# Linear attention and a gated two-layer product on one core: the openings of the slabs interleaved, the last head pairs of batches 0 and 1 woven into them, batch 1's queries loaded beside w_out

## The chip, the cores and the metric

The kernel runs on one core of a Trainium2 chip. The metric is the device time of one execution in microseconds (us), as the median of several runs. The engines are TensorE (PE), VectorE (DVE), ScalarE (ACT), GpSimd (POOL) and SyncE (SP); each works through its own instructions in order and waits on semaphores for the others.

## The reference

```python
def _attn_ref(q, k, v):                       # (8, 8, 576, 64) each
    q_s = np.exp(q - max over d); q_s /= sum over d
    k_s = np.exp(k - max over s); k_s /= sum over s
    kv = np.einsum('bhsd,bhse->bhde', k_s, v)
    return np.einsum('bhsd,bhde->bhse', q_s, kv)

def _moe_ref(x, w_in, w_out, beta):           # x (4608, 512)
    h = x @ w_in                              # (4608, 2048)
    g = h * (1.0 / (1.0 + np.exp(-beta * h)))
    return g @ w_out                          # (4608, 512)
```

The attention's output is laid out as `(batch * seq, head * d)` and is the `x` of the second part.

## The kernel before, in words

The 4608 tokens are nine slabs of 512. Slab t below 8 holds the first 512 tokens of batch t; slab 8 holds the last 64 tokens of all eight batches. Heads are worked in four pairs (`hp`), and a pair is one of the four 128-row pieces `m` of `x`.

Attention of a batch: `exp_q`, `exp_k`, `exp_kr` on ACT (an Exp table), `norm_main` (a reduction and a reciprocal on VectorE, then a multiplication on VectorE or GpSimd) makes EQ, which is transposed into QT: by TensorE and a copy (`t_steps`) in batches 0 to 2, by a DMA transpose on SP's queue (`norm_turn`, `turn`) later. `cast_v` and `cast_vr` turn V to bf16 with a column of ones. `kv_steps` multiplies EK by VB, then VectorE's reciprocal and `kvd` scale and mask it into KVD. `out_mm` (in `out_step`) multiplies KVD by QT, and ACT or VectorE copies the bank into XT, the `x` of the slab.

The product of a slab has two passes. Pass 1 makes 16 tiles: `pass1_tile` accumulates four matmuls of 128x512 (one for each `m`) in one of three PSUM banks (`HB`, L217), ACT applies Silu into GT and `scale_g` divides by beta on VectorE. Pass 2 of slab 0 is `pass2_group`: 16 pieces `f` times four token groups in banks 3 to 6, copied out by `o2_evac`. Pass 2 of every other slab is `pass2_fast`: a scheme of seven products in place of eight, with sums `g_sum1`, `g_sum2` (GS1, GS2), differences `g_diff`, and `w_sum`, `w_diff` of w_out on VectorE; seven groups of 16 matmuls of 256 columns.

What comes when is written out by hand. Every pass-1 matmul is a slot (`tick`), and pass 2 counts 64 slots more, so a slab has 128; a list `todo` for each slab holds steps of the next batch's attention with the slot at which they are put into TensorE's stream (`attn_late` for batches 2 to 4, `attn` later). In `pass2_fast`, hooks `on(n, ...)` run before the n-th product and put work of other engines (exps, norms, casts, loads) into their queues. In slab 0 the loads, exps, sums and norms of batch 1 are put in front of pass 2:

```python
                load_main("qf", qt_h, QF, 1, split=4, after=P.writer[("wout", 11, 0)])
                ...
                exp_q(1)
                w_sum(0)
                w_sum(2)
                for hp in range(NHP):
                    norm_main(1, hp, 1, POOL if hp else DVE)
                cast_vr_s(1)
```

The weights come in on GpSimd's DMA queue (four w_in parts, then four w_out chunks of four `f`), everything else on SP's. The `warm` matmuls of zeros keep TensorE at work in the head.

Of the kernel before, what the change touches and what calls it, by code (L numbers as in the profile page):

```python
# [8 lines left out]
ALU = mybir.AluOpType  # L9
# [145 lines left out]
def bass_efficient_attn_shen__then__act_swish_beta_kernel(  # L155
# [12 lines left out]
    with ExitStack() as es:  # L168
# [187 lines left out]
        def cast_vr(b, hs=(0, 1)):  # L356
            pi = (b // 2) % 2
            for h in hs:
                o = bass.AP(VR[pi][h], 64 * h * NHP * VW, [[NHP * VW, 64], [VW, NHP], [1, 128]])
                a = bass.AP(VRF, 64 * h * 512, [[512, 64], [128, NHP], [1, 128]])  # L360
                add(POOL, lambda e, o=o, a=a: e.tensor_copy(o, a),
                    r=[("vrf", h), ("vrone", pi, h), ("vr0", pi, h)], w=[("vr", pi, h)])
# [144 lines left out]
        def attn_late(b):  # L507
            x = []
            for hp in range(NHP):
                x += out_step(b, hp, MB, ACTE if hp % 2 else DVE)  # L510
            k01, k23 = kv_steps(b, (0, 1)), kv_steps(b, (2, 3))
            if b == 2:
                s = spread(t_steps(b, (0, 1), MB, ACTE), 104, 107) + spread(k01, 107, 110)
                s += spread(k23, 110, 113) + [(113.5, lambda: g_diff(1))] + spread(x[0:2], 114, 116)
                s += spread(t_steps(b, (2, 3), MB, ACTE), 116.5, 119)
                return s + spread(x[2:4], 122, 125)
            if b == 3:
                s = spread(k01, 97, 101) + spread(k23, 101, 105) + [(105, lambda: g_diff(1))]
                return s + spread(x[0:2], 110, 113) + spread(x[2:4], 120, 123)
            return spread(k01, 93, 97) + spread(k23, 97, 101) + spread(x, 105, 122)  # L520
# [55 lines left out]
        load_win(0, 512)  # L576
        norm_main(0, 2, 1, DVE)
        cast_vr_s(0)
        norm_main(0, 3, 1, POOL)
        for c0 in range(512, DFF, 512):  # L580
            load_win(c0, c0 + 512)
# [20 lines left out]
        exp_k(0, 3, 1)  # L602
        cast_v(0, 3, DVE)
        go(kv_steps(0, (1,), HEAD))
# [3 lines left out]
        warm(2, 0)  # L608
        go(out_step(0, 1, HEAD, ACTE))
        go(kv_steps(0, (3,), HEAD))  # L610
        go(out_step(0, 2, HEAD, ACTE))
        go(out_step(0, 3, HEAD, DVE))
# [6 lines left out]
        def pass1_tile(t, f, tick):  # L619
            bk = HB[hrot[0] % 3]  # L620
            hrot[0] += 1
            x = XT8 if t == 8 else XT[t % 2]
            for m in range(NM):
                rd = [("xt8", p_) for p_ in range(4)] if t == 8 else [("xt", t % 2, m)]
                mm(PS[bk][:, :], WIN[:, m, 128 * f:128 * f + 128], x[:, m, :], m == 0,
                   m == NM - 1, r=rd + [("win", f)], w=[("ps", bk)], bk=bk)
                tick()
            add(ACTE, lambda e: e.activation(GT[:, f, :], PS[bk][:, :], ACT.Silu,  # L628
                                             scale=BETA[:, f:f + 1]),
                r=[("ps", bk), "beta"], w=[("gt", f, 0), ("gt", f, 1)], bank=[bk])  # L630
# [53 lines left out]
        def w_sum(n):  # L684
            x, y = (((0, 0), (1, 1)), ((0, 0), (0, 1)), ((1, 0), (1, 1)))[n]
            add(DVE, lambda e: e.tensor_tensor(WSUM[n][:, :, :], quarter(*x), quarter(*y),  # L686
                                               ALU.add),
                r=wkeys(*x) + wkeys(*y), w=[("ws", n)])
# [7 lines left out]
        def pass2_fast(t, tick, hooks):  # L696
# [25 lines left out]
            def wsum(n):  # L722
                return lambda i: WSUM[n][:, i, :], lambda i: [("ws", n)]
# [40 lines left out]
            if t not in (1, 2):  # L764
                g_diff(0)
                g_diff(1)
# [14 lines left out]
        def pass2_group(t, us, bks, tick):  # L781
            for f in range(NF):
                for u, bk in zip(us, bks):
                    mm(PS[bk][:, :], GT[:, f, 128 * u:128 * u + 128], WOUT[:, f, :], f == 0,
                       f == NF - 1, r=[("gt", f, 0), ("gt", f, 1), ("wout", f, 0), ("wout", f, 1)], w=[("ps", bk)], bk=bk)
                    tick()

        NOW = (0, 1, 2, 7)
        for t in range(NSLAB):
            todo = []  # L790
            if t == 0:
                def one(fn, *a):
                    return lambda: fn(*a)

                def steps(fn, *a):
                    return lambda: go(fn(*a))
                todo = [(x, steps(t_steps, 1, (hp,), NOW, ACTE))
                        for hp, x in enumerate((105, 110, 114, 117))]
                todo += [(104, one(exp_kr_s, 1))]
                todo += [(x, one(exp_k, 1, hp, 1)) for hp, x in enumerate((111, 115, 118, 122))]  # L800
                todo += [(x, one(cast_v, 1, hp, DVE)) for hp, x in enumerate((112, 117.5, 120, 125))]
                todo += [(x, steps(kv_steps, 1, (hp,), NOW))
                         for hp, x in enumerate((116, 119, 124))]
                todo += [(x, steps(out_step, 1, hp, NOW, ACTE)) for hp, x in enumerate((121, 126))]
            elif t < 4:
                todo = attn_late(t + 1)
            elif t < 7:
                todo = attn(t + 1)
                if t > 3:
                    todo += spread(outr_steps(2 * t - 5), *((72, 88), (40, 56), (60, 76))[t - 4])  # L810
            elif t == 7:
                todo = spread(outr_steps(1), 32, 48)
# [8 lines left out]
            if t == 1:  # L821
                cast_vr(2)
                for hp in range(NHP):
                    cast_v(2, hp)
                w_diff(0)
                w_diff(1)
            for n in range(NF + 1):
                if n < NF:
                    pass1_tile(t, n if t == 0 else n // 2 + NG * (n % 2), tick)
                if n:  # L830
                    scale_g(n - 1 if t == 0 else (n - 1) // 2 + NG * ((n - 1) % 2))
# [9 lines left out]
                if t == 1 and n in (2, 5, 8, 11):  # L841
                    o2_evac(0, n // 3, 3 + n // 3, ACTE)
                    if n == 11:
                        store(0)
            if t == 0:
                load_main("qf", qt_h, QF, 1, split=4, after=P.writer[("wout", 11, 0)])
# [5 lines left out]
                w_sum(0)  # L852
                w_sum(2)
                for hp in range(NHP):
                    norm_main(1, hp, 1, POOL if hp else DVE)
                cast_vr_s(1)
                pass2_group(0, (0, 1, 2, 3), (3, 4, 5, 6), tick)
                while todo:
                    todo.pop()[1]()
                go(kv_steps(1, (3,), NOW))  # L860
                go(out_step(1, 2, NOW, ACTE))
                go(out_step(1, 3, NOW, DVE))
# [17 lines left out]
            def casts(b):  # L880
                if b % 2 == 0:
                    cast_vr(b)
                for hp in range(NHP):
                    cast_v(b, hp)

            if t == 1:
                on(0, exps, 2)
                on(0, load, 4)
# [13 lines left out]
            elif t == 3:  # L902
# [3 lines left out]
                on(3, norm_turn, 5, 0)  # L906
                on(4, norm_turn, 5, 2)
# [54 lines left out]
```

## Time and profile before

| | |
|---|---|
| median of 9 runs | 284.74 us (284.08 to 284.93) |
| the profiled execution's own time | 285.0 us |
| its span, first to last instruction | 283.2 us |
| mean granted TensorE clock | 0.999 |
| busy: TensorE, VectorE, ACT, GpSimd | 270.2, 194.8, 186.2, 68.0 us |
| pass 1 of slab 0 begins | 15.83 us |
| slab 1, slab 2, slab 3, slab 4 begin | 50.04, 81.07, 110.80, 140.62 us |
| matmul 128x512 of pass 1, 576 of them | 0.379 us each, overlapping |
| Silu of one tile on ACT, 144 of them | 0.688 us |
| scaling of one tile on VectorE, 144 of them | mean 0.388 us |
| Silu or Exp table load on ACT | 1.283 us |

The span is the time between the first and the last instruction; the device time has a little around it. A matmul's record runs from its start to its modelled end, and the next one starts before that, so the busy share of TensorE is higher than the share of its peak. In the tables of stretches, each row has the length, then for each engine the busy time and the number of instructions, the granted clock, the share of the 16 DMA engines (their overlapping packets can take it past 1) and GB/s.

### The profile page before, as it was taken

How to read it: one execution, taken by the hardware profiler on the slowest of the kernel's cores; microseconds unless marked ns; L12 is line 12 of the kernel's file. 1: busy time of each engine (PE TensorE's matmuls, PEld its weight loads, DVE VectorE, ACT ScalarE, POOL GpSimd, SP SyncE). 2: the span in 40 equal slices, each digit the busy share in tenths (PEclk: the TensorE clock that was granted, in tenths of full speed). 3: DMA queues.
4: the chain of work that ended last, by engine and by line, in shares of the span. 5: the costliest groups of instructions: out<-in, count | busy, mean ns of one | idle time of the engine just before them, and what ended most of it. 6: DMA issues, size and time to landing. Idle time of an engine off the chain costs nothing.

```text
span 283.2 us, 4705 instructions
## 1 busy us (share of the span) xinstructions
PE 270.2 (95%) x1845; PEld 168.2 (59%) x1845; DVE 194.8 (69%) x408; ACT 186.2 (66%) x284; POOL 68.0 (24%) x84
## 2 busy tenths in 40 slices
PE   8999997998999989999899999999999999999994
PEld 2544443447854676458654785478548844874583
DVE  4944484688766798787758795869587649634851
ACT  5787566899378875786777956795675477028610
POOL 2790041060611078200810546004200100000000
PEclk9999999999999999999999999999999999999999
DMA  7999999989991029940499999201800130002005
GB/s 219 315 205 202 236 317 344 241 251 380 325 299 51 0 39 247 298 163 0 76 295 258 319 325 160 94 3 37 241 2 0 21 148 0 2 36 112 2 8 140
DMA packets 57205, 45.39 MB, mean 160 GB/s; under 512 B 26448, under 2 KB 56160, under 8 KB 56160
## 3 DMA queue, kind: packets, MB, share of 16 engines
q1 hardware_dynamic: 52352, 40.38, 50.8%
q0 software_dynamic: 4224, 4.19, 9.0%
q10 hardware_dynamic: 608, 0.53, 0.5%
q8 instruction: 14, 0.23, 0.3%
q14 instruction: 7, 0.06, 0.1%
HBM read 36.71 MB, written 9.44 MB: 163 GB/s over the span
## 4 chain that ended last, share of the span: by engine, by line
PE 71%; DVE 12%; DMA 7%; POOL 6%; ACT 1%; issue 1%; POOLq 0%; DVEq 0%
PE PS L375 40%; PE PS L704 30%; DMA WOUT<-in_moe_w_out_dram 6%; POOL EQ L333 4%; DVE GT L634 2%; DVE QS L331 2%; DVE GS L667 2%; DVE GS L662 2%; DMA QT<-EQ 1%; POOL WIN L549 1%; DVE WSUM L686 1%; DVE GT L674 1%; POOL WOUT L555 1%; ACT GT L628 1%; ACT QT L393 1%
## 5 line engine op out<-in xcount | busy, mean ns | idle before, releaser
L375 PE MATMUL PS<-XT,WIN 128*128 128x512 bf16 x576 | 129.9, 379 | 0.9 <-DVE XT L455 0.8
L628 ACT ACTIVATE GT<-PS,BETA 128x512 bf16<-128x512 f32 x144 | 98.7, 688 | 37.7 <-PE PS L375 37.7
L375 PEld LDWEIGHTS PS<-XT,WIN 128*128 128x128 bf16 x576 | 53.8, 98 | 62.2 <-DVE XT L455 1.9
L634 DVE TENSOR_SCALAR GT<-GT,RB 128x512 bf16<-128x512 bf16 x144 | 53.5, 388 | 39.0 <-ACT GT L628 38.6
L333 POOL TENSOR_TENSOR EQ<-EQ,QI 128x1024 bf16<-128x1024 bf16 (+1 forms) x17 | 29.9, 1758 | 94.0 <-DVE QI L332 73.6
L704 PE MATMUL PS<-WOUT,GT 128*128 128x256 bf16 x256 | 33.6, 273 | 0.0
L704 PE MATMUL PS<-WSUM,GT 128*128 128x256 bf16 x256 | 32.0, 273 | 0.1
L704 PE MATMUL PS<-WOUT,GS 128*128 128x256 bf16 x256 | 30.4, 273 | 0.0
L704 PEld LDWEIGHTS PS<-WSUM,GT 128*128 128x128 bf16 x256 | 24.9, 98 | 4.1 <-issue 0.2
L704 PEld LDWEIGHTS PS<-WOUT,GT 128*128 128x128 bf16 x256 | 24.9, 98 | 3.4
L704 PEld LDWEIGHTS PS<-WOUT,GS 128*128 128x128 bf16 x256 | 24.6, 98 | 3.4
L734 ACT COPY O2S<-PS 128x512 f32<-128x512 f32 x16 | 9.4, 586 | 24.9 <-PE PS L704 22.2
L667 DVE TENSOR_TENSOR GS<-GT 128x512 bf16<-128x512 bf16 (+2 forms) x32 | 22.3, 697 | 0.0
L300 ACT ACTIVATE EQ<-QF 128x512 bf16<-128x512 f32 x32 | 17.9, 619 | 6.0 <-DMA QF<-in_q_dram 5.9
L375 PE MATMUL PS<-VB,EK 128*128 128x129 bf16 x128 | 20.7, 220 | 0.7 <-DVE VB L348 0.5
L331 DVE TENSOR_REDUCE QS<-EQ 128x16 f32<-128x1024 bf16 (+1 forms) x20 | 19.7, 987 | 0.0
L455 ACT CAST XT<-PS 128x512 bf16<-128x512 f32 x18 | 10.4, 583 | 13.9 <-PE PS L375 13.9
L674 DVE TENSOR_TENSOR GT<-GT 128x2048 bf16<-128x2048 bf16 x16 | 19.3, 1239 | 0.0
L742 DVE TENSOR_TENSOR O2S<-TS,PS 128x512 f32<-128x512 f32 x16 | 10.7, 679 | 12.2 <-PE PS L704 12.2
L348 POOL CAST VB<-VF 128x512 bf16<-128x512 f32 x24 | 16.1, 670 | 9.6 <-DVE GT L634 7.8
L300 ACT ACTIVATE EK<-KF 128x512 bf16<-128x512 f32 x32 | 18.1, 621 | 0.0
L704 PE MATMUL PS<-WSUM,GS 128*128 128x256 bf16 x128 | 16.7, 273 | 1.4 <-DVE GS L662 1.3
(77 smaller groups left out, 241.7 us busy)
## 6 DMA issues: line engine op xcount, KB each, us to landing
out_dram<-O2S SPq DMA_DIRECT2D x8, 1024.0 KB, 4.9
QF<-in_q_dram SPq DMA_DIRECT2D x6, 1024.0 KB, 7.0
KF<-in_k_dram SPq DMA_DIRECT2D x6, 1024.0 KB, 8.7
VF<-in_v_dram SPq DMA_DIRECT2D x6, 1024.0 KB, 11.8
KF<-in_k_dram SPq DMA_DIRECT2D x8, 256.0 KB, 4.9
VF<-in_v_dram SPq DMA_DIRECT2D x8, 256.0 KB, 5.1
WIN<-in_moe_w_in_dram POOLq DMA_DIRECT2D x4, 512.0 KB, 6.9
WOUT<-in_moe_w_out_dram POOLq DMA_DIRECT2D x4, 512.0 KB, 14.6
```

Of the source, the lines that this page charges most:

```text
L300: add(ACTE, lambda e, o=o, a=a: e.activation(o, a, ACT.Exp), r=[(name + "f", i, hp)], w=[("e" + name, i, hp)])
L331: add(DVE, lambda e: e.tensor_reduce(s_, a, AX.X, ALU.add), r=ks, w=[("qs", i, hp0)])
L333: add(eng, lambda e: e.tensor_tensor(a, a, vb, ALU.mult), r=ks + [("qi", i, hp0)], w=ks)
L348: add(eng, lambda e: (e.copy if eng == ACTE else e.tensor_copy)(o, a), r=[("vf", i, hp), ("vone", i)], w=[("vb", i, hp)], after=after)
L375: add(PE, lambda e: e.matmul(o, l, r_, start=start, stop=stop), r=r, w=w, bank=[bk])
L455: add(eng, lambda e: (e.copy if eng == ACTE else e.tensor_copy)(XT[i][:, hp, :], PS[bk][:, :]), r=[("ps", bk)], w=[("xt", i, hp)], bank=[bk])
L628: add(ACTE, lambda e: e.activation(GT[:, f, :], PS[bk][:, :], ACT.Silu, scale=BETA[:, f:f + 1]), r=[("ps", bk), "beta"], w=[("gt", f, 0), ...
L634: add(DVE, lambda e: e.tensor_scalar(GT[:, f, :], GT[:, f, :], RB[:, f:f + 1], None, ALU.mult), r=k + ["rb"], w=k)
L667: add(DVE, lambda e: e.tensor_tensor(GS2[:, i:i + n, :], GT[:, i:i + n, :], GT[:, i + NG:i + NG + n, :], ALU.add), r=[k_ for f in (i, i + ...
L674: add(DVE, lambda e: e.tensor_tensor(gv(f, th, NG), gv(f, th, NG), gv(f, 1 - th, NG), ALU.subtract), r=gk(f, 0, NG) + gk(f, 1, NG), w=gk(f ...
L704: add(PE, lambda e, l=l, r_=r_, st=st, u=u, i=i: e.matmul(PS[bk][:, 256 * u:256 * u + 256], l, r_, start=st, stop=end and i == NG - 1, ski ...
L742: add(DVE, lambda e: e.tensor_tensor(o, ts, bank3(bk), ALU.add), r=["ts", ("ps", bk)], w=w, bank=[bk])
```

## The change

1. `pass1_lead`: each slab's first three tiles share their `m` order. From slab 1 on the order is m = 0 for tiles 0, 1, 2, then m = 1 and so on; slab 0 has an order of its own (`LEAD0`). The fourth tile uses bank 3, which is an `OB` bank.
2. The copy-in of batch 0's last pair, `out_step(0, 3)`, is at slot 2 of slab 0; batch 1's `out_step(1, 2)`, `kv_steps(1, (3,))` and `out_step(1, 3)` are at slots 1, 3 and 6 of slab 1, with the two `w_diff` behind them.
3. The first w_in load is cut in two halves of 256 columns; the second is issued after the last `norm_main` of batch 0. One `warm` matmul goes, and `kv_steps(0, (1,))` stands ahead of a cast.
4. Batch 1's QF load waits for w_out's first chunk instead of its third. `w_sum(0)` and `w_sum(2)` are halved; the second halves stand behind `norm_main(1, 0)` and `(1, 1)`. The norms of pairs 2 and 3 are all on VectorE, and the slots of batch 1's steps in slab 0 are new.
5. `pass2_group` interleaves its four banks over the first 12 `f` only, then finishes bank by bank. The first `o2_evac` moves to slot 117 of slab 0.
6. Casts of V in the hooks of `pass2_fast` wait for the last GS2 of the slab; batch 2's casts move from the start of slab 1 to its hook 0.
7. In `attn_late` slots of `out_step` move later (batches 2 and 3); for batch 4, `kv_steps` move one slot earlier and `g_diff(1)` goes to slot 100. In slab 3 `g_diff(0)` is at hook 3, and the two `norm_turn` of batch 5 go from hooks 3 and 4 to 4 and 5.

```diff
-        def cast_vr(b, hs=(0, 1)):
+        def cast_vr(b, hs=(0, 1), after=()):
...
-                return s + spread(x[2:4], 122, 125)
+                return s + spread(x[2:4], 123, 126)
             if b == 3:
                 s = spread(k01, 97, 101) + spread(k23, 101, 105) + [(105, lambda: g_diff(1))]
-                return s + spread(x[0:2], 110, 113) + spread(x[2:4], 120, 123)
-            return spread(k01, 93, 97) + spread(k23, 97, 101) + spread(x, 105, 122)
+                return s + spread(x[0:2], 117, 120) + spread(x[2:4], 124, 127)
+            s = spread(k01, 92, 96) + spread(k23, 96, 99.8) + [(100, lambda: g_diff(1))]
+            return s + spread(x, 107, 123)
...
-        load_win(0, 512)
+        load_win(0, 256)
         norm_main(0, 2, 1, DVE)
         cast_vr_s(0)
         norm_main(0, 3, 1, POOL)
+        load_win(256, 512)
...
+        go(kv_steps(0, (1,), HEAD))
         cast_v(0, 3, DVE)
-        go(kv_steps(0, (1,), HEAD))
         warm(2, 0)
         go(out_step(0, 0, HEAD, ACTE))
         go(kv_steps(0, (2,), HEAD))
-        warm(2, 0)
         go(out_step(0, 1, HEAD, ACTE))
+        warm(1, 0)
         go(kv_steps(0, (3,), HEAD))
         go(out_step(0, 2, HEAD, ACTE))
-        go(out_step(0, 3, HEAD, DVE))
...
+        LEAD0 = ((0, 0), (1, 0), (0, 1), (1, 1), (0, 2), (1, 2), (2, 0), (2, 1), (2, 2),
+                 (0, 3), (1, 3), (2, 3))
+        LEAD = tuple((n, m) for m in range(NM) for n in range(3))
+
+        def pass1_lead(t, fs, tick):
+            bks = [HB[(hrot[0] + n) % 3] for n in range(3)]
+            hrot[0] += 3
+            for n, m in LEAD if t else LEAD0:
+                pass1_mm(t, fs[n], m, bks[n])
+                tick()
...
-            if t not in (1, 2):
+            if t > 3:
                 g_diff(0)
                 g_diff(1)
...
         def pass2_group(t, us, bks, tick):
+            ub = list(zip(us, bks))
+            for f, u, bk in ([(f, u, bk) for f in range(12) for u, bk in ub]
+                             + [(f, u, bk) for u, bk in ub for f in range(12, NF)]):
...
                 todo = [(x, steps(t_steps, 1, (hp,), NOW, ACTE))
-                        for hp, x in enumerate((105, 110, 114, 117))]
-                todo += [(104, one(exp_kr_s, 1))]
-                todo += [(x, one(exp_k, 1, hp, 1)) for hp, x in enumerate((111, 115, 118, 122))]
-                todo += [(x, one(cast_v, 1, hp, DVE)) for hp, x in enumerate((112, 117.5, 120, 125))]
+                        for hp, x in enumerate((97, 106, 114, 119))]
+                todo += [(107, one(exp_kr_s, 1))]
+                todo += [(x, one(exp_k, 1, hp, 1)) for hp, x in enumerate((108, 115, 120, 125.5))]
+                todo += [(x, one(cast_v, 1, hp, DVE if hp else POOL))
+                         for hp, x in enumerate((115, 118.5, 123, 127))]
                 todo += [(x, steps(kv_steps, 1, (hp,), NOW))
-                         for hp, x in enumerate((116, 119, 124))]
-                todo += [(x, steps(out_step, 1, hp, NOW, ACTE)) for hp, x in enumerate((121, 126))]
+                         for hp, x in enumerate((118, 122, 126))]
+                todo += [(x, steps(out_step, 1, hp, NOW, ACTE)) for hp, x in enumerate((121, 125))]
+                todo += [(117, one(o2_evac, 0, 0, 3, ACTE))]
+                todo += [(2, steps(out_step, 0, 3, HEAD, DVE))]
...
+                if t == 1:
+                    todo += [(1, steps(out_step, 1, 2, (3,), ACTE)),
+                             (3, steps(kv_steps, 1, (3,), (7,))),
+                             (6, steps(out_step, 1, 3, (7,), DVE)),
+                             (6.1, one(w_diff, 0)), (6.2, one(w_diff, 1))]
...
-            if t == 1:
-                cast_vr(2)
-                for hp in range(NHP):
-                    cast_v(2, hp)
-                w_diff(0)
-                w_diff(1)
...
-                if t == 1 and n in (2, 5, 8, 11):
+                if t == 1 and n in (4, 7, 10):
...
-                load_main("qf", qt_h, QF, 1, split=4, after=P.writer[("wout", 11, 0)])
+                load_main("qf", qt_h, QF, 1, split=4, after=P.writer[("wout", 3, 0)])
...
-                w_sum(0)
-                w_sum(2)
-                for hp in range(NHP):
-                    norm_main(1, hp, 1, POOL if hp else DVE)
+                w_sum(0, 0, 4)
+                w_sum(2, 0, 4)
+                norm_main(1, 0, 1, DVE)
+                norm_main(1, 1, 1, POOL)
                 cast_vr_s(1)
+                w_sum(0, 4, 4)
+                w_sum(2, 4, 4)
+                norm_main(1, 2, 1, DVE)
+                norm_main(1, 3, 1, DVE)
                 pass2_group(0, (0, 1, 2, 3), (3, 4, 5, 6), tick)
                 while todo:
                     todo.pop()[1]()
-                go(kv_steps(1, (3,), NOW))
-                go(out_step(1, 2, NOW, ACTE))
-                go(out_step(1, 3, NOW, DVE))
...
             def casts(b):
+                g = P.writer[("gs2", NG - 1)]
                 if b % 2 == 0:
-                    cast_vr(b)
+                    cast_vr(b, after=g)
                 for hp in range(NHP):
-                    cast_v(b, hp)
+                    cast_v(b, hp, after=g)
 
             if t == 1:
                 on(0, exps, 2)
+                on(0, casts, 2)
...
-                on(3, norm_turn, 5, 0)
-                on(4, norm_turn, 5, 2)
+                on(3, g_diff, 0)
+                on(4, norm_turn, 5, 0)
+                on(5, norm_turn, 5, 2)
```

## The prediction

> **What bounds the kernel now.** I read the page first, then a table of stretches cut at every pass, then the waits and the timeline inside the stretches where TensorE was idle, and last the DMA queues.
>
> ```profile
> PE 270.2 (95%) x1845; PEld 168.2 (59%) x1845; DVE 194.8 (69%) x408; ACT 186.2 (66%) x284; POOL 68.0 (24%) x84
> ```
>
> TensorE is the bound. Back to back, its matmuls of 512 columns start 0.216 us apart, those of 256 0.108 (64 matmuls of pass 1 start between 81.23 and 95.05). The change takes away one matmul (a warm-up), so only idle time can be won. Where it lies (us, then busy per engine):
>
> ```profile
> 29.95:50.04 20.09, 17.73 (x105) 8.32 (x104) 12.27 (x28) 12.22 (x20) 3.79 (x4) 1.00 1.06 308
> ...
> 63.87:81.23 17.36, 16.19 (x154) 13.08 (x153) 13.39 (x28) 11.25 (x19) 4.66 (x2) 1.00 1.08 344
> ...
> 95.05:110.96 15.91, 14.71 (x137) 12.19 (x136) 13.06 (x25) 11.12 (x19) 9.25 (x9) 1.00 0.35 73
> ...
> 124.77:140.62 15.85, 14.53 (x138) 12.11 (x136) 11.59 (x23) 11.34 (x20) 5.47 (x5) 1.00 0.17 26
> ...
> 155.56:169.74 14.18, 13.67 (x126) 11.61 (x125) 12.40 (x21) 10.72 (x18) 6.65 (x8) 1.00 1.06 323
> ```
>
> These are the second passes of slabs 0 to 4: they hold the idle time (the columns after the length are TensorE, its weight loads, VectorE, ACT, GpSimd, clock, DMA share, GB/s). Slab 7's, from 240.48 to 252.85, is busy for all of its 12.37. A matmul counts as busy past the next one's start, so a wait costs more than its idle entry; from start to start the losses are 3.45 (slab 0), 2.29, 1.86, 1.96 and 0.83 us. What ended them, from the chain of waits:
>
> ```profile
> 16.94 17.30 DMA WOUT<-in_moe_w_out_dram
> 34.34 2.36 DVE WSUM L686 x2
> ...
> 49.29 0.70 DVE XT L455
> ...
> 105.74 3.14 DMA QT<-EQ
> ...
> 130.88 2.27 DVE GT L674 x2
> 133.15 1.14 DVE QS L331
> ```
>
> In slab 0 everything of batch 1 queues on VectorE behind the sums of w_out, whose last chunk lands at 34.24; at the end TensorE stands still for batch 1's last two head pairs (X ready at 49.99, pass 1 starts 50.04). In slab 2 `out_mm` waits for the DMA transposes, in slab 3 for KVD behind two differences and a reduction. In slabs 1 and 4 pass 2 opens late, for this (VectorE):
>
> ```profile
> 60.72 2.73 DVE L634 TENSOR_SCALAR GT<-GT,RB 128x512 bf16<-128x512 bf16 x4
> ...
> 91.03 0.87 DVE L634 TENSOR_SCALAR GT<-GT,RB 128x512 bf16<-128x512 bf16 x3
> ```
>
> The first row is beside GpSimd casts (VR, VB from 57.95 to 63.3), the second in slab 2 without them: 0.68 against 0.29 us each.
>
> **Head and pass 1 of slab 0.** One `warm` goes, `kv_steps(0,(1,))` stands ahead of a cast on DVE, and `out_step(0,3)` is woven in after two matmuls. Before: KVD of pair 3 ends at 15.55, its matmul is at 15.60, the first tile at 15.83, and 0.30 is lost at 16.5 for XT of pair 3. After: `out_step(0,2)` near 14.87 as now (KVD of pair 2 still decides), then the lead at 15.09; pass 1 would end at 15.09 + 65 x 0.216 = 29.13, not 29.95: 0.82 won. Against it: the first w_in load is halved. GpSimd issues the second half only at 12.17, after cast and scaling, and each later w_in and w_out issue slides by one issue (0.9). The first half's data is through by 13.7; the first load showed packets at 12.25, 1.9 after its issue ended (10.39), so the second half would start near 15.0, leaving the queue 1.2 idle. The Trainium skill ("DMA: Bandwidth & Descriptors", Specifications) gives about 1 us to the first byte of a GpSimd-issued DMA; by it the hole would be 0.5. I take the trace's row and keep 0 to 1.3. The load for tiles 4 to 7 lands at 12.17 + 6.0 + 1.25 = 19.4, wanted at 18.76: 0.69 given back. Left: **+0.13**.
>
> **Pass 2 of slab 0.** w_out chunks landed at 26.64 (14.74 + 11.9), then every 2.53; now 1.2 later. SP's queue (four QF loads, then krf, vrf, K, V, batch 2) is released by chunk 0, not chunk 2. How do two queues share?
>
> ```profile
> q1 hardware_dynamic: 11, 0.01, 68.9%
> q0 software_dynamic: 10, 0.01, 42.2%
> ```
>
> This is the stretch from 33.0 to 33.1, the end of w_out beside the first QF packets: one packet for one. Alone, a q0 packet takes 96 ns (827 packets at 124.1% of 16 engines in 28 to 32), a q1 packet 44 to 48. One for one leaves w_out two thirds of its pace. The same skill page (Queues, rings and completion order) says that an engine goes round its queues a whole packet of some 9 to 17 descriptors at a time; this rule speaks against the change, as w_out is what the sums wait for. If equal numbers of descriptors are drained it gives the same two thirds; if equal time, half. With QF data from 29.1: chunk 1 at 31.0, chunk 2 at 34.8 (36.7 at half), chunk 3 at 38.5; QF's parts at 31.5 to 38. The sums are split, so norm_main(1,0) waits for chunk 2 only: two half sums (1.35), reduce, reciprocal, multiply (1.55, row 36.70 to 38.25) make EQ ready at 37.8. Its transposes moved from slot 105 to 97 (29.8 + 33 x 0.216 = 36.95): a stall of 0.9. Pair 1 (GpSimd, 39.75) meets slot 106 at 40.0; pairs 2 and 3 follow chunk 3 (40.05 after the sums, then 41.55 and 43.05) and meet 114 and 119 at 41.95 and 43.5. The cast of V and VRS on GpSimd end at 41.3, before slot 118 (43.0). Regrouped `pass2_group` wants chunk 3 at 41.5. KVD behind a cast: 0.15. Losses fall from 3.45 to 1.05: **+2.40**.
>
> **Slab 1.** The lead runs out(1,2), kv(1,3), out(1,3) (0.70 of work, moved, not removed). ACT must finish exp_k and the Silu table load (1.28 + 0.2) before it copies XT of pair 2 (49.4); XT of pair 3 comes at 50.05; some 0.65 is lost against no wait. Twelve matmuls are done at 50.75, before at 52.63: cumulative 1.88. ACT's first silu starts at 50.5; 16 x 0.688 + 3 x 0.58 = 12.75 makes it end near 63.3, before 64.75 (the first o2 copy, 0.58, has moved into slab 0, where ACT waits for TensorE). With casts gone from pass 1 and `w_diff` done by 52.4, VectorE's last sum follows 0.8 later (64.1) where it took 1.8: pass 2's wait ends 2.3 sooner than 66.61. **+0.42**. Casts now follow the last `gs2`: 64.75 + 1.56 + 2.65 (slab 4's and 2's rows) = 69.0, while QI is ready at 68.6; the multiply ends at 71.0, and slot 104 comes at 70.55: 0.3 more wait than before. For this the skill ("SBUF — State Buffer", Who interferes with whom) makes the later of a VectorE instruction with two SBUF inputs and a reading GpSimd instruction block; a reduction never does. VectorE's opening of pass 2 is PSUM reads and reductions, so by it the uncontended rows hold; at the contended rows (1.78 + 3.46) the wait is 1.3. Later out slots save 0.2: **-0.10**.
>
> **Slab 2.** Out slots 110, 120 become 117, 124. The transposes land at 106.05 and 108.89 regardless. Slot 117 is reached at 106.2: 1.10 gone; slot 124 at 108.06: waits 0.87, before 0.43. After it 4 slots remain, not 8 (0.19 each): **+0.67**.
>
> **Slab 3.** `g_diff(1)` goes behind kv, the norms one hook later. RC and KVD end at 133.7, before slot 107 (134.1); both waits go. The late XT of pair 2 (139.2) is needed by matmul 7 of the lead (140.2). SP passes transposes, then load(6), 2 us later; slab 5's batch has a slab of cover; without it the exps wait those 2 us. **+1.65**.
>
> **Slab 4.** Casts after `gs2`: the three contended sums (0.73, 0.96, 0.58 instead of 0.29, 0.7, 0.29) shrink: **+0.60**.
>
> **The lead elsewhere.** Three silus come at once, the first 1.0 later; ACT gains 0.176 per tile (0.864 against 0.688) and is level by tile 8. Table loads fit under the lead. Nothing.
>
> Sum: 0.13 + 2.40 - 0.65 + 0.42 - 0.10 + 0.67 + 1.65 + 0.60 = 5.1. The profiled execution took 285.0 (span 283.2), 0.26 over the median 284.74; subtracted there, **279.6**. About 0.2% (0.6 us) is what a measurement can tell from no change.
>
> **Rivals.** (1) Given back: the stages are each late by turns, GpSimd casts at contended rates (-1), half share (-1.9), a DVE queue order that I misplaced in slab 3 (-1): 1 to 3 us won, 282.5. For it: each slab hangs on three engines. Against: the waits in slabs 2 to 4 have separate causes. (2) Slower: SP's queue starves w_out. Each microsecond that chunk 2 is later is paid whole, through sums, norms and slot 97. The 3.8 us of w_out still ahead of chunk 2 take 5.7 at two thirds; below about 35% share they take 11, which eats all 5.1; at 25% they take 15: 289, and chunk 3 then stops `pass2_group` too. The packet row speaks against it. (3) The lead is not absorbed: were ACT at 0.78 per silu, it would stay 1 us late at each pass's end, 8 us in all, 287; the row of 0.688 is steady. (4) No w_in hole: 278.4.
>
> **Numbers.** The forecast case (with 4) 0.62, its own range 278.2 to 281.2; given back 0.25; slower 0.11; no change 0.02. Range 278.0 to 283.0: it leaves out the slower cases (0.11), no change (0.02) and the far third of the given-back case.
>
> **What would show it.** Right: no wait at 49 to 50; slab 3's pass 2 within 0.3 of dense; slab 1's POOL casts after 64; WSUM halves on DVE at about 35 and 38.6. Wrong: chunk 2 later than 37, ACT with no idle before tile 10 in slabs 2 to 8, or slab 1's transposes waiting over 1 us for EQ.

## The result and the profile after

The changed kernel takes 281.67 us (median of 10 runs, 280.25 to 282.87) against 284.79 for the kernel before in the same series (31 runs, 284.08 to 285.58): ratio 0.9891, 95% interval 0.9878 to 0.9905, so 3.1 us faster. The profiled execution took 282.18 and has a span of 280.4, 2.8 under the span before. The changed kernel's runs lie further apart than those before: the two above 282.8 show a mean granted clock of 0.994, the other eight 0.998 to 1.000, and in e1 below nine of 16 runs are of that kind (0.991 to 0.994, 283.2 to 284.8 us) beside seven at 281.1 to 282.2 (median 281.8).

The page's line of busy times, and the table of stretches cut at the passes as before (length, busy time per engine, clock, DMA share, GB/s):

```profile
PE 269.6 (96%) x1844; PEld 168.2 (60%) x1844; DVE 193.2 (69%) x411; ACT 182.6 (65%) x284; POOL 65.4 (23%) x84
```

```profile
14.90:31.84 16.94, 14.33 (x67) 6.12 (x65) 6.47 (x18) 12.03 (x18) 6.66 (x17) 1.00 1.16 186
31.84:48.12 16.28, 16.28 (x98) 7.92 (x97) 12.15 (x26) 10.53 (x19) 2.87 (x3) 1.00 1.10 307
48.12:63.31 15.19, 15.12 (x72) 6.50 (x71) 11.47 (x27) 13.16 (x22) 0.00 (x0) 1.00 1.07 291
63.31:79.40 16.09, 15.83 (x153) 13.07 (x152) 12.14 (x23) 11.01 (x18) 8.33 (x8) 1.00 1.06 360
...
122.38:136.58 14.20, 14.20 (x137) 12.26 (x135) 11.20 (x23) 11.29 (x20) 2.54 (x2) 1.00 0.00 1
...
151.86:166.73 14.87, 13.65 (x126) 11.50 (x124) 11.25 (x20) 10.75 (x18) 6.29 (x8) 1.00 0.99 284
```

Four stretches tell the story. Slab 0's second pass (31.84 to 48.12) has no idle time where it had 2.36 us of it, and slab 3's (122.38 to 136.58) none where it had 1.32. But slab 0's first pass now takes 16.94 us with 2.61 idle, and slab 4's second pass is idle for 1.22. Two of TensorE's three longest waits name both (us in total, how often, longest), and so does the chain of waits:

```profile
PE PS L376 <- DMA WIN<-in_moe_w_in_dram: 2.6, 1, 2.6
PE PS L376 <- DMA QTR<-EQR: 1.2, 1, 1.2
```

```profile
13.14 8.28 DMA WIN<-in_moe_w_in_dram
21.47 17.66 PE PS L376 x81
...
104.06 3.19 DMA QT<-EQ
...
140.45 1.84 SPq L268
142.33 4.11 SPq L275
146.49 1.35 SPq L275
147.88 1.41 SPq L275
149.33 1.61 SPq L275
150.99 4.00 DMA QTR<-EQR
```

The first new wait is for the part of w_in for tiles 4 to 7, which is issued at 13.14 and lands at 21.42: TensorE stands still before tile 4, and from start to start 2.78 us are lost. The second is a queue: SP issues batch 6's loads one after the other from 139.1, issues of 1.4 to 4.1 us each among them, and only at 150.99 the transpose of the remainder, QTR, which slab 4's `outr_steps` (the products for the last 64 tokens of two batches) want at slot 72 (153.6). There 1.38 us are lost from start to start. Neither row was in the chain before. The transpose in slab 2 is still there, later in the slab.

By slab, start to start, with the 0.70 us of work that moved from slab 0 to slab 1 counted where it was:

| | before | after | won | predicted |
|---|---|---|---|---|
| head and pass 1 of slab 0 (to pass 2) | 29.95 | 31.84 | -1.89 | +0.13 |
| pass 2 of slab 0 | 20.09 | 16.98 | +3.11 | +2.40 |
| slab 1 | 31.03 | 30.58 | +0.45 | -0.33 |
| slab 2 | 29.73 | 29.00 | +0.73 | +0.67 |
| slab 3 | 29.82 | 28.18 | +1.64 | +1.65 |
| slab 4 | 28.95 | 30.15 | -1.20 | +0.60 |
| slabs 5 to 8 | 113.63 | 113.65 | 0.0 | 0 |

The rows won sum to 2.8, the difference of the two spans.

### The profile page after: what moved, and what is told of

Same layout as the page of the kernel before. It is cut to its first block, busy times and chain, and to the rows that moved or that the text cites. A ratio compares the mean times of both kernels' runs of the same rounds, so it can differ in the third digit from the quotient of the medians.

```text
span 280.4 us, 4706 instructions
## 1 busy us (share of the span) xinstructions
PE 269.6 (96%) x1844; PEld 168.2 (60%) x1844; DVE 193.2 (69%) x411; ACT 182.6 (65%) x284; POOL 65.4 (23%) x84
## 4 chain that ended last, share of the span: by engine, by line
PE 77%; POOL 7%; DMA 6%; SPq 4%; DVE 4%; issue 1%; ACT 0%; POOLq 0%
PE PS L376 49%; PE PS L723 27%; POOL EQ L333 4%; SPq L275 3%; DMA WIN<-in_moe_w_in_dram 3%; DMA QTR<-EQR 1%; DVE QS L331 1%; DMA QT<-EQ 1%; POOL VB L348 1%; SPq L268 1%; PE PS L374 1%; POOL VR L361 0%; DVE GT L692 0%; POOL WIN L551 0%; DVE QI L332 0%
## 5 line engine op out<-in xcount | busy, mean ns | idle before, releaser
L627 ACT ACTIVATE GT<-PS,BETA 128x512 bf16<-128x512 f32 x144 | 95.4, 689 | 42.3 <-PE PS L376 41.7
L652 DVE TENSOR_SCALAR GT<-GT,RB 128x512 bf16<-128x512 bf16 x144 | 51.7, 380 | 41.3 <-ACT GT L627 40.9
L333 POOL TENSOR_TENSOR EQ<-EQ,QI 128x1024 bf16<-128x1024 bf16 (+1 forms) x15 | 28.0, 1866 | 70.2 <-DVE QI L332 69.4
L348 POOL CAST VB<-VF 128x512 bf16<-128x512 f32 x25 | 15.5, 622 | 26.0 <-DVE GS L685 14.9
```

The source lines that it names most:

```text
L333: add(eng, lambda e: e.tensor_tensor(a, a, vb, ALU.mult), r=ks + [("qi", i, hp0)], w=ks)
L348: add(eng, lambda e: (e.copy if eng == ACTE else e.tensor_copy)(o, a), r=[("vf", i, hp), ("vone", i)], w=[("vb", i, hp)], after=after)
L652: add(DVE, lambda e: e.tensor_scalar(GT[:, f, :], GT[:, f, :], RB[:, f:f + 1], None, ALU.mult), r=k + ["rb"], w=k)
```

## Experiments

Two theories stood against each other for each new wait. For w_in: halving the part slows the queue (size), or issuing the second half late does (order). For slab 4: the transpose only stands badly in SP's queue, or the queue as a whole is late and carries the delay on. The other runs ask what each piece of the change is worth.

**e1_turn_first: QTR ahead of the loads on SP.**

```diff
-                on(5, load, 6)
                 on(7, norm_turn_rem)
                 on(7, load_rem, "qrf", qt_h, QRF, 4)
+                on(7, load, 6)
```

> In slab 3 the transpose of the remainder (QTR) and the QRF loads are issued by SP before the loads of batch 6 instead of behind them. Theory (slab 4's new wait is SP's queue: the transpose stands behind eleven microseconds of load issues that now begin later against TensorE): the wait of 1.39 us for QTR at the third group of slab 4's pass 2 goes to below 0.1, slab 4 takes about 28.8 us instead of 30.15, the whole is 1.2 to 1.4 us faster than the changed kernel, near 280.4. Rival (the loads of batch 6 are then late instead, and the exps and casts of slab 4's second pass take the wait over): no more than 0.4 us faster, with TensorE waiting for VB, EK or QT later in slab 4 or in slab 5.

Measured: 283.32 us, ratio 0.9939 (0.9917 to 0.9962), slower than the changed kernel. The wait for QTR in slab 4 is gone and slab 4 takes 28.98 instead of 30.15. Slab 5 then takes 30.19 instead of 28.41; the waits between 167 and 180:

```profile
PE PS L376 <- DMA QTR<-EQR: 1.6, 1, 1.6
```

The rival is right: the loads, two microseconds later, push the next remainder's transpose back to 178.71, ahead of which slab 5's products stand. Slab 4 wins 1.17 us and slab 5 loses 1.78. The larger part of the lost time lies in slab 0, which this edit does not touch. In the profiled execution the w_in wait there costs 3.14 us instead of 2.78, and after it TensorE was granted half its clock, as the fourth digit of the page's row shows (each digit is a fortieth of the span; first e1, then the changed kernel):

```profile
PEclk9997999999999999999999999999999999999999
```

```profile
PEclk9999999999999999999999999999999999999999
```

From 23.04 to 26.45 us the clock is 0.50, and the matmuls of 512 columns start 0.43 us apart instead of 0.216: another 1.6 us. So pass 2 of slab 0 begins at 33.83 instead of 31.84. Without these 2.0 us the kernel would be within 0.5 us of the changed one. The w_in wait, and what follows it, differs from run to run.

**e2_whole_win: the first w_in part whole.**

```diff
-        load_win(0, 256)
+        load_win(0, 512)
...
-        load_win(256, 512)
```

> The changed kernel with the first w_in load whole, as before the change; all else as changed. Theory (halving the load slows GpSimd's DMA queue itself, so that tiles 4 to 7 get their weights at 21.4): the part for tiles 4 to 7 lands near 18.2, the wait of 2.8 us before tile 4 goes, some 0.7 us is lost at 15 instead since the lead needs the whole part (15.6), and pass 1 of slab 0 ends near 30.0 instead of 31.8. Of these 1.8 us some is lost again in pass 2 of slab 0, where the norms of batch 1 hang on w_out: between 0.7 and 1.8 us faster than the changed kernel. Rival (the wait is of that one execution, or slab 0's end hangs on w_out's last chunk whatever pass 1 does): within 0.4 us of the changed kernel.

Measured: 279.71 us (279.34 to 279.79), ratio 0.9820 (0.9804 to 0.9837), 2.0 us faster than the changed kernel and with a narrow spread. The part for tiles 4 to 7 lands at 18.18, TensorE waits 0.9 at the lead instead, slab 0 ends at 45.83 instead of 48.12. The rival is out. Size and order of the halves both remain; the next run parts them.

**e3_halves_together: both halves, issued one behind the other.**

```diff
         load_win(0, 256)
+        load_win(256, 512)
         norm_main(0, 2, 1, DVE)
         cast_vr_s(0)
         norm_main(0, 3, 1, POOL)
-        load_win(256, 512)
```

> The changed kernel with the second half of the first w_in part issued directly behind the first half (before the cast and the scaling of GpSimd), so that only the size of the halves is left and not the late issue. If the smaller packets are the cause: the part for tiles 4 to 7 still lands after 20.5 and TensorE still waits over 2 us before tile 4. If the late issue of the second half is the cause: it lands by 19 and the wait is below 0.5 us; but EQ of pair 3 of batch 0 comes about 1 us later from GpSimd, so that the lead starts later by up to 1 us.

Measured: 279.73 us, ratio 0.9825 (0.9809 to 0.9841). The part for tiles 4 to 7 lands at 18.49 and TensorE has no wait for w_in at all; the lead begins 0.68 us later (15.58). So it is the late issue, not the size of the halves. GpSimd's DMA queue between 16 and 19 us, from the DMA view (packets, MB, share of the 16 engines), first in the changed kernel, then in this one:

```profile
q0 software_dynamic: 385, 0.39, 91.6%
```

```profile
q0 software_dynamic: 613, 0.61, 124.0%
```

In the same three microseconds these are 385 packets of 1 KB against 613, or 128 GB/s against 204. The mean pace is not the whole of it. In e1 and e4, which have the same late issue, the queue moved 156 and 184 GB/s in this stretch, and the part still came late. The trace holds 16 landing records for each load, and TensorE can start only after the last of them. For the part for tiles 4 to 7:

| | first of 16 | the middle two | last of 16 | GB/s, 16 to 19 us |
|---|---|---|---|---|
| e3 (halves together) | 18.21 | 18.28, 18.32 | 18.49 | 204 |
| changed kernel | 18.83 | 19.57, 19.67 | 21.42 | 128 |
| e1 (same late issue) | 18.44 | 18.72, 18.73 | 21.73 | 156 |
| e4 (same late issue) | 18.36 | 18.63, 18.66 | 20.38 | 184 |
| e7 (next run) | 18.52 | 18.80, 18.84 | 20.76 | 180 |

With the late issue some of the 16 shares of the load fall two to three microseconds behind the others, and TensorE waits for the slowest. They stay behind: the first w_out load lands between 26.94 and 29.06 in the changed kernel.

**e7_cut_384: the late cut at column 384.**

```diff
-        load_win(0, 256)
+        load_win(0, 384)
...
-        load_win(256, 512)
+        load_win(384, 512)
```

> The changed kernel with the first w_in part cut at column 384 instead of 256, the second piece issued late as changed. Theory (the loss comes from GpSimd's DMA queue running empty before the second piece's descriptors are there, after which it runs at 115 to 150 GB/s for six microseconds; the first piece of 384 columns lasts until about 14.2, when the second is there): the queue keeps about 200 GB/s, the part for tiles 4 to 7 lands by 19, TensorE waits less than 0.5 us before tile 4, about 279.7 as with the halves together. Rival (any piece issued that late slows the queue, or small packets do): it lands after 20 and the wait is over 1.5 us, above 281.

Measured: 280.62 us, ratio 0.9865 (0.9851 to 0.9878). The wait is 2.1 us and the part for tiles 4 to 7 lands at 20.76. My theory, that the queue only has to be kept from running empty until the second piece comes, fell. Between 13 and 14 the queue moves 206 GB/s, so it did not run empty there, and between 16 and 19 it is at 180, yet the last of the 16 landings is 2.3 us behind e3's. This run does not separate the late issue from small packets: its second piece of 128 columns comes in packets of 256 bytes, where the halves have 512, and the pace is lowest (69 GB/s, from 15 to 16) around its end. Why the late issue leaves some shares behind stays open.

**e4_qf_at_chunk2 and e6_halves_qf_chunk2: the query loads released by the third chunk again**, once on the changed kernel and once on e3.

```diff
-        load_main("qf", qt_h, QF, 1, split=4, after=P.writer[("wout", 3, 0)])
+        load_main("qf", qt_h, QF, 1, split=4, after=P.writer[("wout", 11, 0)])
```

> The changed kernel with batch 1's query loads released by w_out's third chunk, as before the change. Theory (one packet for one between the two queues, and the early queries are what lets the norms start): w_out's last chunk lands near 37 instead of 39.4, the queries at 37.5 to 40.5, the first norm ends about 39.5 instead of 37.9, after slot 97: 0.5 to 1.2 us slower than the changed kernel. Rival (the queries starve w_out, which is what slab 0 hangs on): 0.5 to 1.5 us faster, with the last two norms of batch 1 some 2 us earlier.

> The kernel with the halves together, and batch 1's query loads released by w_out's third chunk as before the change. Theory (one packet for one, the early queries start the norms): w_out's last chunk lands near 34.5 instead of 37.3, the queries near 35 to 38, the first norm ends near 37.5 to 38, 1.5 to 2 us after slot 97, and pass 2 of slab 0 loses 1 to 2 us more: 0.8 to 1.8 us slower than with the halves together. Rival (w_out slowed by the queries costs as much as the early queries bring): within 0.4 us or faster.

Measured: e4 282.91 us (ratio 0.9942, 0.9922 to 0.9962), 1.2 slower than the changed kernel, though in another series; e6 281.50 (0.9897, 0.9884 to 0.9911), 1.8 slower than e3. The first has a w_in wait of its own size (1.96) and a stall of 1.25 at slot 97; e6, without a w_in wait, decides. w_out's last chunk lands at 35.78 instead of 37.30, as expected, and yet pass 2 stands still for 1.9 us at slot 97. VectorE in e6, then in e3:

```profile
37.14 0.69 DVE L331 TENSOR_REDUCE QS<-EQ 128x8 f32<-128x512 bf16 x1 [3.32 <-ACT EQ L300]
37.86 0.20 DVE L332 RECIPROCAL QI<-QS 128x8 f32<-128x8 f32 x1
38.10 0.69 DVE L333 TENSOR_TENSOR EQ<-EQ,QI 128x512 bf16<-128x512 bf16 x1
```

```profile
34.39 0.69 DVE L331 TENSOR_REDUCE QS<-EQ 128x8 f32<-128x512 bf16 x1
35.11 0.20 DVE L332 RECIPROCAL QI<-QS 128x8 f32<-128x8 f32 x1
35.35 0.69 DVE L333 TENSOR_TENSOR EQ<-EQ,QI 128x512 bf16<-128x512 bf16 x1
```

The bracket in the first line says it: VectorE, its sums done, waits 3.32 us for the exp, hence for the queries. The early query loads cost w_out 1.5 us that nobody misses, and bring the first norm 2.75 us forward.

**e5_outr_late and e8_tile_order.** e5 is e3 with `outr_steps` of slab 4 at slots 110 to 126; e8 is e5 with the first three tiles of slabs 2 to 8 one after the other.

```diff
-        *((72, 88), (40, 56), (60, 76))[t - 4]
+        *((110, 126), (40, 56), (60, 76))[t - 4]
```

```diff
-            for n, m in LEAD if t else LEAD0:
+            for n, m in (LEAD0, LEAD, sorted(LEAD))[min(t, 2)]:
```

> The kernel with the halves together, and slab 4's remainder products (the first users of QTR) at slots 110 to 126 of their slab instead of 72 to 88; SP's queue is as changed. Theory (slab 4's loss is only that these products stand in TensorE's stream ahead of the landing of QTR, near 152.8; SP's order itself costs nothing): the wait of 1.1 us in slab 4 goes and nothing takes its place, slab 4 takes about 29.0 us instead of 30.1, and the whole is about 1.1 us faster than with the halves together: 278.6. Rival (SP's queue carries the delay on, as it did when the transpose was put ahead of the loads): slab 5 waits for QTR or QT as much as slab 4 gained, 279.5 or more.

> The kernel of the late remainder products, with the first three tiles of slabs 2 to 8 one after the other again (slots and banks as changed). Theory (the m-by-m order only gives the last head pairs of X time, in the slabs whose out steps moved late; its burst of three silus costs nothing): TensorE waits 0.3 to 0.9 us at the first tiles of slabs 2 and 3 for X of pairs 2 and 3 and nowhere else, 0.5 to 1.5 us slower than the late remainder products. Rival (the burst delays ACT and its tile order is better): faster, with ACT's last silu of slabs 5 to 8 earlier.

Measured: 292.77 us (ratio 1.0285, 1.0271 to 1.0299) and 293.22 (1.0306, 1.0289 to 1.0323). The slot was badly chosen: hook 5 comes at slot 109.7 and queues the next remainder's transpose into QTR, so from slot 110 on the products read the next remainder and not their own (in these two kernels that part of slab 8's x comes from other rows), and TensorE waits for it:

```profile
PE PS L376 <- DMA QTR<-EQR: 11.2, 1, 11.2
```

During this wait the granted clock fell to 0.50, from 163.3 to 177.0 us in e5, which lengthens slab 4 further.

As a test of slab 4 this failed. The pair still answers e8's question, as both have the same fault: slab by slab, slabs 2 and 3 take 29.00 and 28.18 us in e5, 29.04 and 28.18 in e8, and slabs 5 to 8 are equal to 0.02. Neither theory held: from slab 2 on the m-by-m order of the lead neither helps nor costs. My expectation that it buys time for late X was wrong: in e8 TensorE has no wait for X at the first tiles of slabs 2 and 3.

**f1_outr_92: the same products at slots 92 to 108**, ahead of hook 5 (on e3).

```diff
-        *((72, 88), (40, 56), (60, 76))[t - 4]
+        *((92, 108), (40, 56), (60, 76))[t - 4]
```

> The kernel with the halves together, and slab 4's remainder products at slots 92 to 108: behind the landing of QTR (about 152.8, slot 92 comes near 155.5) and still ahead of hook 5, which queues the next remainder transpose into the same tile. Theory (slab 4's loss is that these products stand in TensorE's stream ahead of the landing): the wait of 1.1 us goes, slab 4 takes about 29.0 us, no new wait in slab 5, the whole 1.0 to 1.2 us faster than with the halves together: 278.6. Rival (SP's queue carries the delay on into slab 5, as when the transpose went ahead of the loads): within 0.4 us of the halves together, with a wait for QTR in slab 5.

Measured: 279.15 us (278.87 to 279.62), ratio 0.9807 (0.9788 to 0.9826): the lowest median of all, 5.3 us under the kernel before and 2.5 under the changed one (0.6 under e3, from another series, with overlapping intervals). Slab 4 takes 28.98 and slab 5 28.41, without a wait for QTR in either. So SP's order costs nothing once its user stands later. In the traces slab 4 is 1.10 shorter than in e3 (30.08), and slab 0 is 0.7 longer, with waits of 0.62 and 0.43 at the transposes of pairs 0 and 1. The edit does not touch slab 0; over e3, e5, e8, f1, f2 and f3, in which slab 0 is the same, it takes 30.65 to 31.34. So part of what the medians (0.6) leave of the 1.1 may be chance.

The last three runs each take one piece of the change off f1.

**f2_casts_free: casts in the hooks without waiting for GS2.**

```diff
-                g = P.writer[("gs2", NG - 1)]
+                g = ()
```

> The kernel with the remainder products at 92, and the casts in the hooks no longer waiting for the last GS2 of the slab (they stay in their hooks). Theory (the casts of slab 1 and slab 4 then run on GpSimd beside VectorE's sums and slow them, as before the change): the last sums of slab 1 and slab 4 stretch (0.29 to about 0.6), pass 2 waits for GS again, 0.7 to 1.2 us in slab 1 and 0.4 to 0.7 us in slab 4, less 0.3 us at slab 1's transposes whose scaling then finds GpSimd free: 0.8 to 1.6 us slower than with the casts held. Rival (nothing hangs on these sums now): within 0.3 us.

Measured: 280.13 us, ratio 0.9840 (0.9823 to 0.9858), 1.0 slower. Slab 1 takes 32.17 instead of 31.28, with waits of 1.2 us in all for GS; slab 4 is unchanged at 28.98. VectorE in slab 1, f2 and then f1:

```profile
60.20 0.77 DVE L680 TENSOR_TENSOR GS<-GT 128x512 bf16<-128x512 bf16 x1
60.90 1.09 DVE L685 TENSOR_TENSOR GS<-GT 128x1024 bf16<-128x1024 bf16 x1
```

```profile
60.15 0.42 DVE L680 TENSOR_TENSOR GS<-GT 128x512 bf16<-128x512 bf16 x1
60.50 0.68 DVE L685 TENSOR_TENSOR GS<-GT 128x1024 bf16<-128x1024 bf16 x1
```

Beside GpSimd's casts the same sums take 0.77 and 1.09 instead of 0.42 and 0.68. So holding the casts is worth 0.9 us in slab 1 and nothing in slab 4.

**f3_slab3_old: slab 3's order as before.**

```diff
-            s = spread(k01, 92, 96) + spread(k23, 96, 99.8) + [(100, lambda: g_diff(1))]
-            return s + spread(x, 107, 123)
+            return spread(k01, 93, 97) + spread(k23, 97, 101) + spread(x, 105, 122)
...
-                on(3, g_diff, 0)
-                on(4, norm_turn, 5, 0)
-                on(5, norm_turn, 5, 2)
+                on(3, norm_turn, 5, 0)
+                on(4, norm_turn, 5, 2)
```

(and the differences of slab 3 in front of hook 3 again)

> The kernel with the remainder products at 92, and slab 3's order (kv and out slots of batch 4, both differences, hooks of batch 5's norms) as before the change. Theory (the order in slab 3 is worth what its waits for KVD were): slab 3's pass 2 waits 1.4 us and 0.3 us for KVD again and takes about 29.8 us instead of 28.2, nothing is given back in slab 4 since the remainder products no longer hang on SP: 1.4 to 1.7 us slower. Rival (SP's queue gains what slab 3 loses, transposes and loads being issued earlier): less than 1 us slower.

Measured: 280.96 us, ratio 0.9868 (0.9851 to 0.9886), 1.8 slower. Slab 3 takes 29.83 instead of 28.17: 1.66, with the losses of 1.6 and 0.27 at KVD back, the larger of them this row:

```profile
PE PS L722 <- DVE KVD L418: 1.4, 1, 1.4
```

Slab 4 takes 28.62 instead of 28.98: the new order gives 0.36 back, since the casts of batch 5 come later and slab 4's first kv waits for VB (0.34 in f1, none here).

**f4_unwoven: batch 1's last kv and out products at the end of slab 0.**

```diff
-                    todo += [(1, steps(out_step, 1, 2, (3,), ACTE)),
-                             (3, steps(kv_steps, 1, (3,), (7,))),
-                             (6, steps(out_step, 1, 3, (7,), DVE)),
-                             (6.1, one(w_diff, 0)), (6.2, one(w_diff, 1))]
...
+                go(kv_steps(1, (3,), NOW))
+                go(out_step(1, 2, NOW, ACTE))
+                go(out_step(1, 3, NOW, DVE))
+                w_diff(0)
+                w_diff(1)
```

> The kernel with the remainder products at 92, and batch 1's last kv and two out products back at the end of slab 0, in front of slab 1's lead, with the two differences of w_out behind them. Theory (the weave covers KVD and the copies of X with lead matmuls): TensorE waits about 0.6 us for KVD of pair 3 and 0.3 to 1.0 us for X at the lead's later matmuls, of which the woven lead already loses 0.66 us in waits of its own: 0.5 to 1.2 us slower. Rival (slab 1's pass 1 is bound by ACT's silus, which start after the lead in both): within 0.3 us.

Measured: 280.72 us, ratio 0.9859 (0.9838 to 0.9879), 1.6 slower. Slabs 0 and 1 together take 63.67 instead of 62.63: 1.0 in the traces. TensorE waits 0.80 for VB, 0.60 for KVD and 0.71 for X where the woven lead waits 0.44 once. Here the weave earns its place (the two `w_diff` move with it and were not tried alone).

## Why the prediction was right or wrong

The forecast was 279.6, inside a range of 278.0 to 283.0; measured were 281.67, 3.1 us won of 5.1. The direction was right, and so was the mechanism in the second passes of slabs 0 to 3: the waits named there went or shrank. The number lies inside the wide range but outside the forecast case's own range (278.2 to 281.2), next to what had been listed as "given back" (282.5, 1 to 3 us won). By stage, two terms missed by 2.0 and 1.8 us (the head, slab 4), two came out 0.7 and 0.8 better than written (pass 2 of slab 0, slab 1), and two were met.

*Slabs 2 and 3 held to the tenth.* In slab 2 the wait for the second transpose was put at 0.87 and is 0.82; in slab 3 both waits went, and undoing slab 3's order alone (f3) costs 1.66, written as 1.65. In both, one engine's queue decides, and every duration that the sum needed was in a row of the trace.

*Slab 4 is the step that failed.* It said that SP's two microseconds had a slab of cover, and named only the loads of batch 6 and slab 5 as behind them. The same queue holds the QTR transpose behind those loads, and its user is in slab 4's own pass 2. Before, it landed at 156.12 and was used at 157.88: 1.8 us of slack, while the change took 4.0 us off TensorE's way there and moved the landing to 154.98, only 1.1 earlier. e1 and f1, which take the wait away in two ways, both bring slab 4 to 28.98: this is the 1.2 us lost. But 28.98 is no better than the 28.95 before, so the 0.60 put down as won is missing too. Of the three rows named there, the two that are sums did shrink (to 0.29 each; the 0.96 was a row of two scalings), but not because the casts are held: f2 takes the hold off and slab 4 stays at 28.98. There the casts wait for VRF anyway (in f2 the first begins at 152.84, when VRF lands; pass 2 opened at 151.21, and the last sum begins at 152.72), so the earlier opening of pass 2 took the collision away. What was won by it is lost again at the start of the slab: with slab 3's norms one hook later the casts of batch 5 come later, and slab 4's first kv waits 0.34 for VB. Without slab 3's new order (f3) slab 4 takes 28.62.

*The w_in term was mis-sized.* Direction and place were right (tiles 4 to 7 want a part that comes late), 0.69 us was written and 2.78 measured. I had counted a hole of 1.2 in the queue and full pace after it. Weighed there was the trace's 1.9 us from issue to first packet against the Trainium skill's about 1 us ("DMA: Bandwidth & Descriptors", Specifications). The second half, issued by 13.15, landed at 16.48; the first half landed between 13.79 and 14.42, and the queue dipped to about 40 GB/s near 13.75 but had no gap between 13 and 15: nearer to the page's figure than to my row. The cost was neither. It was the next load, whose 16 landings are spread over 2.6 us where e3's lie within 0.3; the cause of that is open.

*Pass 2 of slab 0 was better than written, partly for a bad reason.* The two queues did share one packet for one. From 33 to 35 us, after:

```profile
q0 software_dynamic: 249, 0.25, 73.1%
q1 hardware_dynamic: 251, 0.24, 44.3%
```

In packets w_out kept 60% of the pace that it has alone (827 in 4 us), two thirds written. On "DMA: Bandwidth & Descriptors" (Queues, rings and completion order): a turn by whole packets with equal numbers of descriptors fits these rows, with 1.65 to one in time; equal time for both, which would have meant half the pace, does not.

w_out's third and fourth chunks landed at 34.99 and 39.38 (34.8 and 38.5 written), the first norm ended at 37.86 (37.8). That the third chunk and the norm agree is luck. The first chunk was 1.2 us later than written (29.06, not 27.84), as part of the lag behind the late w_in issue. Against that, the query data came late: issued at 29.08, it shows its first packets at 32.6, not 29.1, so the sharing began 3.5 us later. In e3, without the lag, the third chunk landed at 33.11. The first of the query parts landed at 35.48 instead of 31.5. The predicted stall of 0.9 at slot 97 did not appear because TensorE came 2.0 us later to it, held up by w_in. In e3, where it comes on time (36.8), the norm is done at 36.0, and pass 2, counted as above, takes 17.25 us: 2.84 of the 3.11 won do not hang on the w_in wait.

*Slab 1 was 0.8 better than written.* The lead's own waits were as put down (0.66). But ACT's silus ran closer behind each other than their row's 0.688 (five took 3.00, a step of 0.58 between starts), and VectorE's last sum kept up, so pass 2 lost no more than 0.13 for GS. The casts behind GS2 ran uncontended as reckoned (1.35 and 2.64), ended at 69.5 against 69.0 written, and the transposes waited 0.34 us.

Of the rivals, the starving of w_out did not come (60% of its pace, with the third chunk two microseconds ahead of the 37 named as a sign), and the burst of the lead was absorbed (ACT waits for TensorE again from the seventh tile of each slab from 2 on; e8). "Given back" came closest, by another road than those listed: a queue that the sum had not followed to its end. The signs named for being right came: no loss above 0.23 us around the start of slab 1, slab 3's second pass without idle time, slab 1's casts from 65.38 on, the halves of WSUM from 35.01 and 39.48.

## What to carry to other kernels

When a step is moved on a queue, list everything behind it to the end of the queue and who waits for each landing, and compare the landing with the new, earlier time of its user: slack measured against a slower kernel is gone once the stages before are faster. Where such a transfer comes late, moving its user behind the landing (f1) is worth more than moving the transfer forward in a full queue, which passes the delay on (e1). And watch when the last part of a load lands, not only at the queue's pace: here, putting one issue in late left some shares of the next loads two to three microseconds behind, and issuing the two halves back to back (e3) avoided it.

## What the runs showed of the hardware

- With the second piece of the first w_in load issued late on GpSimd's queue, the 16 landings of the next load were spread over 2.0 to 3.3 us (18.36 to 20.38 in e4, 18.44 to 21.73 in e1; 2.6 in the changed kernel, 2.2 in e7); with the halves issued together over 0.3 (e3, f1), and in e6 one of the 16 came 0.9 behind the rest. The queue moved 128 to 184 GB/s between 16 and 19 us against 204 in e3. The cause is open.
- In e1, after TensorE had stood still for 3 us, its granted clock was 0.50 from 23.04 to 26.45 us, and matmuls of 512 columns started 0.43 us apart instead of 0.216. In the changed kernel's profiled execution a wait of 2.6 us had no such sequel.
- Back to back, the silus of 128x512 start 0.58 us apart although each record is 0.69 long (five from 51.86).
- Query loads released by w_out's first chunk showed their first packets 3.5 to 3.6 us after the issue (the changed kernel, e2, e3, e7); released by its third chunk, with only the last still to come, 1.0 to 1.2 us after it (the kernel before, e4, e6). In the idle start of the kernel it is 1.1 us.
- VectorE's sums of 128x512 and 128x1024 took 0.77 and 1.09 us beside GpSimd's casts (f2), 0.42 and 0.68 without them (f1).
